# Transposes of a two-layer attention and token-MLP kernel, from the full array to four 64x64 tiles

## The chip, the core and the metric

The kernel runs on one core of a Trainium2 chip. The metric is the device time of one execution in microseconds (us). Engines are called as in the profile: PE is the matrix engine, DVE the vector engine, ACT the scalar engine that computes activations, POOL the general engine, SP the engine whose queue starts the loads. PSUM, where PE writes, has eight banks of 512 float32 per partition; bank numbers below are the second index of the tile `ps`.

## The reference

The input x has 2048 tokens of 512 features. Two layers, each of two halves, use the same weights twice:

```python
x = x + _A_ref(_layernorm(x), A_wqkv, A_wo)                # sliding-window attention
x = x + _B_ref(_layernorm(x), B_w1, B_b1, B_w2, B_b2)      # MLP across the tokens
x = x + _A_ref(_layernorm(x), A_wqkv, A_wo)
x = x + _B_ref(_layernorm(x), B_w1, B_b1, B_w2, B_b2)
```

`_A_ref` has 32 heads of 16 features; each token attends to itself and the 255 tokens before it. `_B_ref` multiplies along the tokens (2048 to 1792, gelu, 1792 to 2048) for each feature.

## The kernel before, in words

Tokens lie in 16 tiles of 128 (`x_sb`, and normalised `xh_sb`). Attention goes through four blocks Q of 512 tokens. A block needs its normalised tokens with features on the partitions, `xhT` (two buffers in turn). From it PE computes k, q and v in projections of four 128x128 by 128x512 matmuls (`project`, L591; v at L695). Then there are 36 steps a block (four groups of heads, nine shifts m of the window): `emit_scores` (L795) writes scores into one of two pairs of PSUM banks (0 and 1, or 2 and 3), `emit_exp` (L806) takes the exponential on ACT, an edge mask is multiplied in by DVE or POOL (L823), and `emit_pv` (L844) adds probabilities times values into banks 4 and 5. Scores and values use the array as four independent 64x64 tiles; such operations carry the mode "cells" in the code, the others "full".

All other products of PE during attention share banks 6 and 7: projections, transposes, the normalisation of the output (L887), the output product (L760), and parts of the MLP that are done beside attention (L607). A product occupies its bank from the write until the instruction that empties it has ended.

The first block's four token tiles are transposed one at a time (L567). The later blocks' tiles are transposed in pairs by `job_transpose_two` (L580): two jobs for each of three blocks in each of two layers, twelve jobs in all. One job is eight transposes of 128x128 against the identity, written as bf16 into one bank (8 x 128 x 2 bytes fill it), and one copy of 128x1024 from there to `xhT` (`copy_out`, L440 on DVE or L442 on ACT).

The order of work is written out by hand in tables. The program records operations as jobs, sorted by due time and then put in the sequence `ORDER`; dependencies (who must wait for whom, through tiles and banks) follow from that sequence. `BANKS` has bits for each job that choose bank 6 or 7 for each product. `LINES` gives each engine its list of operations, by their number among all operations in job order, so it also says which engine does an operation that several could do. Each engine runs its list strictly in order (`Plan.emit`) and waits on semaphores where a dependency is on another engine. PE therefore stops at a product whose bank is not yet empty, and all behind it on PE stops too.

Of the kernel before, what the change touches and what calls it, by code (L numbers as in the profile page):

```python
# [29 lines left out]
def _table(*text):  # L30
# [5 lines left out]
    'c-pm-Ne;ju3<DYe|It<36QUtoiNu9qWIOQ~ckvvCUEkdu!hhkTGe1YTP~@rQU0fFp^)x;4x-$AF=Njp%un%%{$-(R<s119<{N!Zp&wOBPJZ2gw'  # L36
    '_#DUKdY*TM)IMraJ>OSnL0d(ACotVqnr}=Y&BW*Olgl)%J+933^`8{tWL?s+0Cx')
ORDER = _table(
    'c-jTQ17Hvc00q#G>{_;$ZQEM5ZQHnPo6ELs+qP}qdjKJXM+g|95E5aK5^)h0kr5i<5E0Q40Z|YM(U1_a5EU^I196Z5fry9Lh>v7Qj6}$YBuIgz'
    'NQ2}^g|x_l)JTU+$d86dkF3ao?8uB_$c1dkgPh2K0OUh%6ht}XMPU>`Q4~TE)I~{@MsZX{36w=CR74q+M<wh-5UQXlDx*58p%yxzChDLDx}gGU'  # L40
    'qdpp=I~t%KnxPR|U?TdWC7Pf$nxidRp$*!jGlrlO+My%5peuS}9@e8bMxh7#qZbCD9|mGHrei1uU^up+4+di-{=*22#TbmoZVbZ&Ou;xD!emUt'
    'RLsO|%)%VZ#SARKB+SPmEJQGt;sh3BIhJ81R^cqxVhuK6HP&GXHen;SVg){9Gqzv{wqqB*;4=1OC-&k14&pwJ;4qHiDQ@5tj^YeX;yCu;JWk^r'
    'F5(jI;R3EAB(LBauHz4G;}-7VChp=P9^eVy;5i=S5uV{CUg0&~;sqk{15)!nKH?odAt}G(D}Lh}e&Hv`4EzBw1pgrnO))gXGXk?R3L`T*OEQ45'
    '7@N^pkx?0!aTt*aS%V1}pNW}_F&K`Cn1m@9ipiOZe-X%(OvAKH$Mg)#{EWve%*f2l#9WNY?99fT%)=ba&AiOVRxHQ@EW*NU$YLDDLM+PSEWu7J'
    '%~CAOaxB9N3}Sg!VI|gLW!7X}R%dNCU>(+DBQ|DzR%J6bXHzy|OSWKJwr3l5VLNtaNA_TEc4K$;Vm}UGPj+Qr4&p!#<zNnDAO6RYoX9a8!PXqd'
    '(HzV1oWRMP!v37eX`IU0oWWU~$N8MZxm?60T*$>-%3!YGYA)wWuHrhb<$7-CHE!TlZsc_i;R5dAGG5^(?&frE;Z5G=X0G8a-rx>y<xXznF7D+%'
    'p5y`U=P4fMSsv$69^?fc;|ZST5uW2Ap5aBF=Oy0ZWj^LzKHz;m;ypg(dp_fHzTi`S<P*N+8@}Z$zUDiA;3t0JAAaR`M$<Qb<}ZfV4~EcB{w4K~'
    'zZpjs6iQM^g;p3vRX9adVue*?MNlN=RSX3vtD-2n;wh$LDYfD%ff6acnkcCfD!Gy<nF3W#sZ>)Ll}<&JM(LGZnbl93ludb*LpfDnxm8g4)k#y8'
    'PlZ)L#Z*W=)LNxgROMAll~h(0RasS3O+yr0HB?o#Rb91IR}EE1jnzQS)JRR$LM@d`DV0H4lveH3M$HwZR_dU(YOgZttZwR}3hJto>aG&%rM~K|'
    '0qUc{>aRf>rjDwo5gMxD8m)mErLh{L@tUC7nxtu3pk<n<8JeP5>Z$3PsX3afd77`)TC9aSpkOW4a;?xv?b0f()EceTIIY(@ZPX@h&=zghHf`52'  # L50
    '?a)r`(QfV4WbM--ZPh^?)(IWaQ61N5oz!`q(J5WjSzXX2UDge~*A?B>65Y{l-PAK(*EQYO13l7H-O@RQ@I$@OW4+Z?J<)T$)JMJ1Ywgz;z0(JM'
    ')=z!XJ^j`Xebq1h(>KBLEB#eS({^ZwaeRkzIEQsaf7c&HaU@4@fFnDaqdTUPI)-CAj^jDJqdJx2I*}7Ni4!`pW4Vk2oy;kn+&P`W>73eWT*zIW'
    '!kL`jX`R&>oyB!r#krls&79r2T*P^t*L_^rrCiL#o!R+a!j)Xs*__YiT+!7X<kGI}f-dTkuIXy7=kl)M`mXDSZsaCz>I!b*R&L|gZtsq6;M#8M'
    '4sPx)uIldY?4IuC9`5DdZs*4C?|vTW0dDCb9_GOw>7gFs;U4309__In?+Kpd$?ofEp5m#V=^38o*<R!W-tRfy>p@=XQQqfep6iL8=fghe`JV1W'
    'KH?=_=mlQvV6XCKZ}Cbm_X=<IHt+NvZ}cXw_Xe-=TCesluk#LX_imr`d7tqmAN4U`^>Lr_37_^2pYuhZ^=)79Jzw!P-}hx-_Z{E#1K;&6KlCF%'
    '_7ndP&4=a!')
LINES = {
    "tensor": _table(
    'c-jrshkFRt769;j?>Xn5dv22ojaH4KjVDIZMA1GJv4a>-(HfPg5yYO!vqzMo)>C_ab`ce|pAa>kM6H_PqgIOw5<!T({t>_LS5bwkN~*G|qN=Je'
    '6|O#35h_wORne-Nicu|8JJnjXQD3M&DnTWw8ETZ8ppw;EHD66p^VA}>O6^e#)i$+KZB!f7Nwq^AP+QecYM(l!Zm1*bjC!JutBdM_%2J|ltE=iy'  # L60
    'bxWO4)72yOhssrD^-J}a%2A|Wr~=hk7uE0TNL@+?>Eb#>m((BXP+duf>)tv{SJ$8DT6&`Xr;gI|bzR+3ch?JaU)@5->4Ey9UaNcQ;W|kV(8F}1'
    '9;=gesve^!>uGw9UZ!(&1+z+T)JODEy;7&>4SJhCs_*EZ^?qI5?9gd?pFXHFb%s8p>zVWVy6$GK>EHED{fB<2|J2#~vCh|5^h;f+-)J_@3^0Kv'
    'zyzDpCdrgH<xHpvF<`2iDkjndnJg1wJ~cH>9dq4uG__3=)7f+}TTCzWjp=Lln?+`*8EN{MA;!QsGs28DlgwnZ*~~Gs&3yA8^TaGOOU+8N!E}IB'
    'v%~B$8Rn4LZPLs!bKIOXr%W+8Z_b&E=8|awcg=cuWbT*;Cf~$Cp?P5}6c~a)cpC=6`%nVPL0JfeN^lgyAq?umC8z-npgDMmg2vDaVxS#7Gyj4w'
    ';VbA0U&Azrg#OSQ5+EMNKnRS0p^yZfa3Una1egNJU~v}Agt>4ZR=^xs4y$1el)z1}5q7~r*aBN29kxLVWWshh1Bc-!$bt+w4OihN?0{6b2RGmj'
    'JcPgCH59;8$bnn{RQL>nFb{(9ITXRt_zsrB7Z8Fkp%Q+Cp%{U+u`JfZy4VaGVhaqzcGwXUFb+Fl0QSUK?1Ayv2NN*~Be5EOg4J;<j>8&Q6F<ez'
    'a0ZUWWc&_i<2)RQOK=dbz{R*62jdzXf~#>e4#i=Zg2QnWZo>n(AJgy=9>NiL7;`We8{q=X#&tLmJ)On^e1mUMCceOzn1$ysA8+7AEW{!dK#%bm'
    '22oK`^aS(p6_%zl6iUHVj*3xn3ZxQLiK<c<g-``5Pw!I%MbhWghU!uSYDm%4oZ8Y58cP4B(G*90DS^6EFN&vuG>XR40GdD}X(p|u*|dPNXg;l='
    'leC!j(sJ5N+v!JILuh}d6#6giqyu!A(&-8vqf=De{zgYBlg?5<dyjsnCf3=@beA5`LkhQS18p%IU@zD*wuCKe-?OFdhjx*zY<Jo^wx%6xtJ_+('
    'xs9@+T;ImqXxqxRw#V&I+uIJXc{Y)!*d*KE4zVL`Nxoy}*`;=}t--79T)WV&vg_>z`<R~47Q5X(r5|k$<<c|SZSyF_?y}G61*O}Uluy6fefAZ-'  # L70
    'rUE)=uh>)eti5b+*qgSU{ld1l9c)MYrTxl2wD)W$+u3%pUG3Mln~k-P?QQ$OX4}^`m<z1pzo|0tdyGtMxg1wuX2<1O*z;Q)z*RVqt8oZd=18u?'
    'x%Q}y;@VuFqdA<LaVw7D_S}`HavYE5xxA6bb1aYI$y|oV@g$zc(|Hzu&%1aLFXUWa%j<Xxr*I>_$*H`9_wjyi%V~U&kMVI%=L|l{m-sS+%i?Q%'
    'n{V+w?!i4dn|pC@e#P<Jhx>9qJ6Fj4SUGkH+@A+<5%;be$b)z=mvV2rcU(#Lfh+66TqpOLtKq7-aM#@Z!!>YCU9g+wVqBE#;2OIS*V4tg_U<Y7'
    'cCoIP8|>=15pIwh?#8-gH{G>$bKNvI(=Bj6xMOaKTkKZ31efU6yX|hJTjx^TPPfaQcL!XWJK~nRO)lMKx-%}ropyU&ExGP4xohsS3zl4$?e4n='
    'uA*#`=Pp1VxjcswFCC<m6qPX&BvquOd?00Iztoh<^07onzI)|jq`K6R*Y0yEa4jWP+Q=K%P72-MSxAEPkZ$sg43vH{REEhYNt6aMUcQrt(n!9S'
    '#xhG5N)u@+YowV(%RE^k>!piqmz}asQY2M&%O068|C1B)tDKSvGEpYUMVTyFazUoZEx9T;Bv~HFRQXo2<-R<Ur;;Q2@=6X$nkaur4ojf~`T!r~'
    ')1|0CBELv6e^g?8C*RGVmAlf)=SgQD>&y6NKH8V_b$vY_;Vb$$|B<ii8~WzHwQuAb`})3%@8Mhco<7RQ`|f_2Z{x@NuD*#M?)&&revqHw6Mcdo'
    '?ECxCevDt>SNo;@2fxA3@H72vKgVzNYy2{w>Ua9RexFbC8~rwa#Q)-t`$Im%XZq9ryg%cA^C$dOf64zJNC^?W'),
    "vector": _table(
    'c-jTQ3seYJ7y#h^{`da(zxOht)uxD&!iXhVGnGSyvYkp|4MQ=^BU2-(jTm`tEU$^fI+*9qMw93`DAPG(^dO{ZUd`-`J?z2k`#ORz_(3P=0xv)Z'  # L80
    '@PW4A30@Ed{h&XDLl{KB02l-w5Dk&w4}-xQ0^l_m2t(jScphRP7P`VP2!sSkfkc=JqoEk`Ar+=W8q9!PcnfC1A{Yw`U<?$%n=lS`!FZSeyI~)c'
    'z(hC(r{FYXKsuy|lW-GKMY4DViJ}@-LXsFQ#)u}k3thx0ktUwO6BsLEMW~3wAmJy1#YpTW#);Q)f_O&^#{psl7KtbkEe45UxI_#U@pwffV1r1+'
    'H*mhl6`5kL*d>mLLh-vu!S$k21mWi*825_<;*Ka26{0^T<7qJ(YeY1@jg#<!_(j|ox5RaEO*|C>XQM+e^u{^35OZ-6DkKa+jqNZK8?illVgwfA'
    'a%{p#T#E-W9am!pj>i*Nfm`rH+>gsp%15{pci?v1i>3G-o<UEUD&yo;tip@<0Ds0`@d-|nLK>MVJ*2PfD9_3OxkvVu4KiG|lC5Qe{1YEznhceN'
    'vY(tS^JJJ@Dd)*7*-fsJ`SJr9B!lG!xk;v}0=Zm%Ebq(D<fpP&7Re6EN9~tKWtps$M`Wq2l`XPP3WbW4xB6H9BVSTol)oCOLexyvMm?t@)T?Tp'
    '`a~6}Vs${BRxv78ZB%ipTJ2U#)E;$FeW41}CACQ{Rh!jeRjMwi^Xix?SB>h1s#Q&@PTf?^s$Tu5uBZleRozl|lplFhPYR(R3LqZ}r6`J~!8DX&'
    'D3;<Wi4tfeCDT00qHG#Psgy#CXe{MXKFy>VG?}JSI%Uu_%A_2cLyKtvt)X4CgbHXKEv1jBk&0+D?VuG@PFv|X71JRieV9t<BvsNi^48T<L$&m-'
    '{)ui=oF1lI={~xx_RyDgR~@Lg=+4?#m+E}oOGoP7Izji~A$q7z)aUeLou#vN4rl85dV%)kJGw}3(BZsIcjQC*gg&l?{*Rs!YN<gt>Ki&;Pt+ND'
    'lAf%mXm4JrSLn5Rjc&v3xILfMp4^r_xDWT`cwWxyc`xU&A9v<ue3Z-h7$4+A9K&C6EGKa?kK$8Y!DqOcFR(I|+`>(KkK_0uSMeqOo`2waM$^i)'
    'HtkFn&*f}>kNwR&exHkZJ4cu>6K{geKvTkAX1LkO1I!LyYr2`=c(RE!gUkme-z1wPv&wvH&Y5a6)66m@X12*O3r()6Gi9d2)SJuZmT5Mp%yv^{'  # L90
    '%1w(IXuWKW`NMR#4@?ic&uTl(PPeJHlg+ce?Fn09U$FtUs|~b?HpxcWXp44^&9vEewH;xL?N&S9j<a9eZ)}m>U^m)wd(}4EoA$OXv@7gG`_xM3'
    '>CW03TWfusue)m>+d6yCc6NTQ#r|dgw%RG@?*g22*1hbyyHMA|1-hQDn+tNiT|XD%`nYfx=BBu8H{C6EIc~0-<?`Gnx5lk=C2pH5b;sRa_ob_H'
    'r`&m0?=HD&cilC({{fr%KFI'),
    "scalar": _table(
    'c-jTQd1x187y#h!J-+w&z?GV;bfy^^ZN{jTQ*0&kkILCh87UoF6H^;%q&ew_xDuN%rFoR)F~%I^RkV@0B(=##iaKSqFl7mvw9I2hBhfK>o>5_1'
    'C=Ij1qR<lRLRDB2GGSx*I8=wv!uHS*_Jwc5>F`}R8rnl=I3K!0f~(<LxE1=s-5@X!hCnvtz*xwIe0U3<fyqz|FT;G;1{Lrgtb`1#foj+cbx;Eh'
    'un(HxXE+2$pcOix6T09MT!CwF8}30s$1EI)WAJf&0-wT(ScG%%P27MBu>x1%Dy+hFxEVjkI^2r~@h~38lXw=pupNKHKk*jc!$3;+(QtZ%aw(sl'
    'r$U-aB{YM|=rx*0OKCAxQij%2H7S2eTd1BIX+Ql$ZPY=X)J>PEhi=jUF%RZpJd($9E<ejt_$8jsWju$=`5k_jGrW|mcs+0At-O=#xseZW6CdS^'
    'T*<4rjZbk4|HXeZ#DDld?&nc)Xv~gTF)!xF$Ks=LL@bC;$2a1pxGmPl9r1MhIyT2c@mOq&C*s-oYwU?vqRWjqRI=nDd06tKND8Gyie<69A}eH>'
    'WaJasD!XL2?3HHuMt+bsIVZo!MY$|Dq(^ScFddKwwN}RHI32GATBLnatkZOc&ed0SwwCK^{Yckojn?XR?bENcNe}7~ZPk-{Mla~^dR2S1U){jE'  # L100
# [242 lines left out]
def bass_interleave_layers__sliding_block__mixer_token_mlp__prompt_kernel(  # L343
# [25 lines left out]
    with es:  # L369
# [202 lines left out]

        def job_transpose_two(Q, i, prio):
            b, t, buf = misc_bank(), 4 * Q + i, Q % 2
            pv = ps[:, b, :].bitcast(dt.bfloat16)

            def f(e):
                for j in range(2):
# [581 lines left out]
```

## Time and profile before

| What | us |
|---|---|
| Median of 3 runs | 504.71 |
| Lowest and highest | 503.58, 505.14 |
| The profiled execution, its own time | 504.01 |
| Its span (first to last instruction of the program) | 502.3 |
| L795 on PE, scores, 2816 matmuls | 108.5 busy |
| L844 on PE, values, 2816 matmuls | 92.1 busy |
| L580 on PE, the changed transposes, 96 matmuls | 7.1 busy |
| L806 on ACT, 288 exps | 261.5 busy |

Busy time counts stretches in which at least one instruction of the group ran; matmuls overlap, so for PE the distance from one start to the next says more than the length of one. The granted clock of PE is 0.999 of full speed throughout. Attention of layer 1 lies from about 14 to 163 us of the span, its MLP to 231 (with its last part beside the next attention), attention of layer 2 to 404, its MLP to the end.

### The profile page before, as it was taken

The numbers are of one execution on the slowest core, as the hardware profiler recorded it, in microseconds if no ns is written. First come the engines' busy times: TensorE is split into PE (matmuls) and PEld (weight loads), VectorE is DVE, ScalarE is ACT, GpSimd is POOL, SyncE is SP. The second block draws the span as 40 slices with busy tenths as digits, with TensorE's granted clock in tenths as the row PEclk, the third lists the DMA queues.
The fourth block names the chain that finished last, engine by engine and source line by source line (L and its number), as shares of the span: only waits on it lengthen the run. The fifth ranks groups of instructions, "written<-read, shape, count | busy, mean of one in ns | idle before, by whom it ended". The sixth has DMA issues, their size and how long they took to land.

```text
span 502.3 us, 19381 instructions
## 1 busy us (share of the span) xinstructions
PE 474.3 (94%) x8385; PEld 272.0 (54%) x8454; DVE 323.4 (64%) x660; ACT 315.6 (63%) x381; POOL 213.1 (42%) x375
## 2 busy tenths in 40 slices
PE   8898989998999999998998999999999999999997
PEld 4454556555766444444444776566547754444444
DVE  7989988887663571366897447878886549131222
ACT  2898999997999314400776669889989960340000
POOL 5897756664564030001874555577544312200000
PEclk9999999999999999999999999999999999999999
DMA  6922222242222725050002140114214256050661
GB/s 209 96 79 84 70 71 77 85 114 68 78 62 70 216 79 147 0 147 1 24 9 61 50 137 15 38 61 136 85 47 114 71 156 185 0 146 12 198 200 52
DMA packets 76516, 44.52 MB, mean 89 GB/s; under 512 B 8976, under 2 KB 75408, under 8 KB 76432
## 3 DMA queue, kind: packets, MB, share of 16 engines
q1 hardware_dynamic: 72560, 43.27, 29.3%
q0 software_dynamic: 3872, 0.02, 1.4%
q8 instruction: 66, 1.08, 0.9%
q14 instruction: 18, 0.15, 0.1%
HBM read 32.51 MB, written 2.10 MB: 69 GB/s over the span
## 4 chain that ended last, share of the span: by engine, by line
PE 70%; ACT 8%; DVE 6%; POOL 6%; issue 4%; DMA 3%; SPq 2%; DVEq 0%; ACTq 0%; POOLq 0%
PE ps L1029 14%; PE ps L983 13%; PE ps L795 9%; PE ps L844 8%; ACT p_sb L806 7%; PE ps L591 7%; PE ps L607 7%; PE ps L760 4%; PE ps L695 4%; POOL p_sb L823 3%; SPq L434 2%; PE ps L519 1%; PE ps L887 1%; DMA w1buf<-in_B_w_dram 1%; POOL xh_sb L544 1%
## 5 line engine op out<-in xcount | busy, mean ns | idle before, releaser
L806 ACT ACTIVATE p_sb<-ps 128x1024 bf16<-128x1024 f32 (+8 forms) x288 | 261.5, 977 | 47.4 <-PE ps L795 39.0
L823 POOL TENSOR_TENSOR p_sb<-p_sb,edge 128x128 bf16<-128x128 bf16 (+2 forms) x263 | 127.4, 491 | 114.1 <-ACT p_sb L806 99.3
L795 PE MATMUL ps<-q_sb,k_sb 64*64 64x288 bf16 (+8 forms) x2816 | 108.5, 249 | 3.4 <-ACT p_sb L806 2.3
L844 PE MATMUL ps<-p_sb,v_all 64*34 64x288 bf16 (+17 forms) x2816 | 92.1, 246 | 4.4 <-issue 1.5
L795 PEld LDWEIGHTS ps<-q_sb,k_sb 64*64 64x64 bf16 x2816 | 60.0, 106 | 46.6 <-ACT p_sb L806 22.6
L844 PEld LDWEIGHTS ps<-p_sb,v_all 64*64 64x64 bf16 (+1 forms) x2816 | 60.0, 100 | 21.5 <-POOL p_sb L823 6.3
L591 PE MATMUL ps<-xhT,wqkv 128*128 128x512 bf16 x214 | 55.4, 380 | 4.8 <-issue 2.7
L823 DVE TENSOR_TENSOR p_sb<-p_sb,edge 128x128 bf16<-128x128 bf16 (+2 forms) x137 | 39.9, 300 | 21.9 <-ACT p_sb L806 14.5
L1033 DVE SCALAR_TENSOR_TENSOR x_sb<-ps,b2col,x_sb 128x512 bf16<-128x512 f32 x23 | 17.1, 750 | 44.4 <-PE ps L1029 43.9
L537 POOL TENSOR_TENSOR rstd<-vare,mhalf 128x4 f32<-128x4 f32 (+1 forms) x17 | 16.6, 977 | 67.1 <-DVE vare L535 53.9
L983 PE MATMUL ps<-xh_sb,w1buf 128*128 128x512 bf16 x186 | 44.1, 379 | 0.6 <-issue 0.5
L525 DVE BATCH_NORM_STATS2 stats<-x_sb 128x6 f32<-128x512 bf16 x64 | 43.0, 681 | 0.6
L710 POOL TENSOR_TENSOR v_all<-vt,even 128x1024 bf16<-128x1024 f32 (+2 forms) x23 | 34.3, 1495 | 17.3 <-DVE vt L698 17.3
L547 ACT ACTIVATE xh_sb<-x_sb,shift,rstd 128x512 bf16<-128x512 bf16 x11 | 8.8, 813 | 50.5 <-POOL shift L541 34.7
L632 DVE TENSOR_TENSOR k_sb<-ps,half 128x1024 bf16<-128x1024 f32 (+1 forms) x32 | 37.3, 1166 | 4.7 <-PE ps L622 2.4
L1029 PE MATMUL ps<-ubuf,w1buf 128*128 128x512 bf16 x165 | 37.4, 379 | 0.2
L607 PE MATMUL ps<-xh_sb,w1low 64*64 64x512 bf16 x512 | 35.5, 377 | 0.1
L1029 PE MATMUL ps<-ubuf,oU 128*128 128x512 bf16 x150 | 34.5, 379 | 0.2
L988 DVE TENSOR_TENSOR ps<-ps,ubuf 128x512 f32<-128x512 f32 x16 | 11.2, 700 | 35.1 <-PE ps L983 35.1
L591 PEld LDWEIGHTS ps<-xhT,wqkv 128*128 128x128 bf16 x240 | 19.5, 98 | 26.5 <-issue 4.4
L695 PE MATMUL ps<-xhT,wqkv 128*128 128x512 bf16 x114 | 30.1, 380 | 3.5 <-issue 1.4
L990 ACT ACTIVATE ubuf<-ps,b1col 128x512 bf16<-128x512 f32 x28 | 19.0, 686 | 22.9 <-DVE ps L988 13.0
(89 smaller groups left out, 531.4 us busy)
## 6 DMA issues: line engine op xcount, KB each, us to landing
w1buf<-in_B_w_dram SPq DMA_DIRECT2D x30, 256.0 KB
w1buf<-in_B_w_dram SPq DMA_DIRECT2D x50, 128.0 KB
oU<-in_B_w_dram SPq DMA_DIRECT2D x18, 256.0 KB
oU<-o SPq DMA_DIRECT2D x16, 256.0 KB
w1low<-in_B_w_dram SPq DMA_DIRECT2D x32, 128.0 KB
q_sb<-qt SPq DMA_DIRECT2D x120, 32.0 KB
xhT<-in_B_w_dram SPq DMA_DIRECT2D x4, 512.0 KB
k_sb<-in_B_w_dram SPq DMA_DIRECT2D x4, 512.0 KB
```

Source lines behind the costliest of these rows:

```text
L525: dve(lambda e: e.bn_stats(stats[:, t, :], x_sb[:, t, :]), 690, prio, reads=[R("x", t)], writes=[R("stats", t)])
L591: last = e.matmul(ps[:, b, :], lhsT=wqkv[:, c, c0:c0 + P], rhs=xhT[:, buf, c, :], start=(c == 0), stop=(c == 3))
L607: last = e.matmul(ps[64 * h:64 * h + 64, banks[r ^ swap], :], lhsT=lhs(r ^ swap, c, rows, 64 * h), rhs=rhs(r ^ swap, c, rows), start=(c == ...
L632: return e.tensor_tensor(dst, src.unsqueeze(2).to_broadcast([P, n, 2, w]), mask[:].unsqueeze(1).unsqueeze(3).to_broadcast([P, n, 2, w]), o ...
L695: last = e.matmul(ps[:, b, :], lhsT=wv[:, c], rhs=xhT[:, buf, c, :], start=(c == 0), stop=(c == 3))
L710: return e.tensor_tensor(dst, src.unsqueeze(2).to_broadcast([P, n, 2, DH]), even[:].unsqueeze(1).unsqueeze(3).to_broadcast([P, n, 2, DH]), ...
L795: last = e.matmul(ps[64 * c:64 * c + 64, 2 * half + r, 32 * i0:32 * i1], lhsT=k_sb[rows, ring, t, kb % 16, :], rhs=q_sb[rows, t, c, 32 * i ...
L806: exps[plan.job] = last_exp[0] = plan.op({ACT: (170 + int(2 * (512 - c0) * 0.84), lambda e: e.activation(p_sb[:, slot, :, c0:512], ps[:, 2 ...
L823: return e.tensor_tensor(v, v, g, op=ALU.mult)
L844: last = e.matmul(ps[64 * r:64 * r + w, B_O + (c ^ r), 32 * i0:32 * i1], lhsT=v_all[rows, pos - 32 * c:pos - 32 * c + w], rhs=p_sb[rows, s ...
L983: r = e.matmul(ps[:, b, :], lhsT=blk[:, sc - 8 * part, (ft % 2) * P:(ft % 2 + 1) * P], rhs=xh_sb[:, sc, :], start=(sc == 8 * part), stop=( ...
L1029: r = e.matmul(ps[:, b, :], lhsT=blk[:, turn[n], (st % 2) * P:(st % 2 + 1) * P], rhs=u_at(turn[n]), start=(n == 0), stop=(n == NFT - 1))
```

## The change

`job_transpose_two` transposes in quarters of the array. For each of the eight 128x128 pieces there are now four transposes of 64x64, one for each row half r and column half h, in the position (64r, 64h) of the array. Row half r writes to its own bank, so a job takes both shared banks, and uses half of each. Each bank is emptied by a copy of 128x512; the two copies can go to different engines. The job's mode is "cells".

```diff
         def job_transpose_two(Q, i, prio):
-            b, t, buf = misc_bank(), 4 * Q + i, Q % 2
-            pv = ps[:, b, :].bitcast(dt.bfloat16)
+            banks, t, buf = (misc_bank(), misc_bank()), 4 * Q + i, Q % 2
+            pv = [ps[:, b, 0:256].bitcast(dt.bfloat16) for b in banks]
 
             def f(e):
                 for j in range(2):
                     for c in range(4):
-                        last = e.transpose(pv[:, (4 * j + c) * P:(4 * j + c + 1) * P], xh_sb[:, t + j, c * P:(c + 1) * P], ident[:])
+                        for r in range(2):
+                            rows, n = slice(64 * r, 64 * r + 64), 64 * (4 * j + c)
+                            for h in range(2):
+                                last = e.transpose(pv[r][64 * h:64 * h + 64, n:n + 64], xh_sb[rows, t + j, c * P + 64 * h:c * P + 64 * h + 64],
+                                                   ident[rows, rows], tile_position=(64 * r, 64 * h))
                 return last
-            pe(f, 450, prio, reads=[R("xh", t), R("xh", t + 1), R("ident")], writes=[BK(b)])
-            copy_out(xhT[:, buf, :, i * P:(i + 2) * P].rearrange("p c (j n) -> p c j n", j=2),
-                     pv.rearrange("p (j c n) -> p c j n", j=2, c=4), b, prio, 750, [R("xhT", buf, i), R("xhT", buf, i + 1)])
+            pe(f, 240, prio, reads=[R("xh", t), R("xh", t + 1), R("ident")], writes=[BK(b) for b in banks], mode="cells")
+            for r, b in enumerate(banks):
+                copy_out(xhT[:, buf, :, i * P:(i + 2) * P].rearrange("p c (j r n) -> p c j r n", j=2, r=2)[:, :, :, r],
+                         pv[r].rearrange("p (j c n) -> p c j n", j=2, c=4), b, prio, 420, [R("xhT", buf, i + r)])
```

The numbers 450, 240, 750 and 420 are the planner's costs in ns; with the tables given they do not act. The tables `BANKS`, `ORDER` and `LINES` are replaced whole. Decoded, they say:

- PE's list has 1004 operations before and after, the same ones; 621 keep their relative order. DVE has 648 operations in place of 660, ACT 381 in place of 372, POOL 386 in place of 371, SP 375 as before.
- Before, the jobs' copies are 11 on DVE and 1 on ACT; after, 21 on DVE and 3 on ACT.
- Counting the new jobs as "cells", PE's list goes from "full" to "cells" and back 100 times before and 90 times after.
- The next product in one of a job's banks, counted in places of PE's list: before, at least 4 places after the job for every job; after, 3 to 5 places for nine jobs, and 6 or 7 for the other three.
- In layer 2, ACT's list has 191 operations in place of 181; in layer 1, 190 in place of 191.

## Prediction, on record before the result was known

> **What bounds the kernel now.** I read the page's engine table first, then the chain of work that ended last, then busy time by stage (before attention, attention of layer 1, its MLP, attention of layer 2, last MLP).
>
> ```profile
> span 502.3 us, 19381 instructions
> ...
> PE 474.3 (94%) x8385; PEld 272.0 (54%) x8454; DVE 323.4 (64%) x660; ACT 315.6 (63%) x381; POOL 213.1 (42%) x375
> ...
> PE 70%; ACT 8%; DVE 6%; POOL 6%; issue 4%; DMA 3%; SPq 2%; DVEq 0%; ACTq 0%; POOLq 0%
> ```
>
> TensorE is busy in 94% of the span and holds 70% of the chain. So work that it no longer does is worth nearly its length, wherever it is not waiting for another engine.
>
> ```profile
> 14.00:163.00 149.00, 138.69 (x3440) 85.62 (x3467) 117.03 (x241) 137.23 (x162) 95.30 (x165) 1.00 0.32 80
> ...
> 231.00:404.00 173.00, 163.62 (x3866) 104.50 (x3893) 126.92 (x248) 138.60 (x161) 93.91 (x161) 1.00 0.22 64
> ```
>
> These are the two attention stages, where all twelve changed jobs lie (columns: length, PE, PEld, DVE, ACT, POOL, granted clock, DMA). In layer 1 PE (138.7) and ACT (137.2 of 149.0) are both nearly full; in layer 2 ACT has 34 us to spare. PE idles 10.3 + 9.4 us in the two.
>
> One changed job in the timeline of PE (start, length, line):
>
> ```profile
> 41.94 0.39 PE L795 MATMUL ps<-q_sb,k_sb 64*64 64x288 bf16 x8
> 42.26 0.62 PE L580 MATMUL ps<-ident,xh_sb 128*128 128x128 bf16 x8
> 42.81 0.30 PE L844 MATMUL ps<-p_sb,v_all 64*34 64x256 bf16 x4
> ```
>
> The job holds PE for 0.55 us from its first start to the next instruction's.
>
> **TensorE's price, from start to start.** Busy times of pipelined matmuls overlap, so I take the records' starts. Eight 128-column transposes start 56 ns apart (median of 119): 8 x 56 = 0.45 us a job. A group of four 64x64 matmuls, one on each quarter of the array, takes 28 ns for 64 columns (145 groups) and 56 ns for 128 (221). The new job is 8 such groups of 64 columns: 8 x 28 = 0.22 us. The saving is 0.224 us a job, 12 jobs: **2.7 us**. The trace has no eight short groups in a row, only single ones between longer ones, so the other end is the 56 ns that the rows of 16 groups at L887 keep up, at which this term is zero. I take 28, since the row has the same tile and the same columns.
>
> The Trainium skill speaks against this. "TensorE: Matmul & The Clock Gate", section "Wait — 56ns, not 53.3ns?", says that matmuls never start closer than about 25 ns, however small. Counted for each of the 32, that is an estimated 0.80 us a job, and the sum below would turn to a loss of about 2 us before any wait. The trace bears it out for groups only: the four matmuls of a 64-column group start within 10 ns (median), and 32-column groups still take 28.
>
> **Changes of mode.** Between quarter tiles and the full array PE loses time beside the pitch: quarter to full 158 ns after a 128-column group, against 56; full to quarter 149 after a transpose, against 56, and 309 after a 512-column matmul, against 216. A pair costs 0.10 + 0.09 = 0.20 us. I decoded the order tables in the diff and walked PE's list: 100 pairs before, 90 after (54 to 51 in layer 1, 46 to 39 in layer 2), since every new transpose job stands between attention steps, which use quarter tiles. 10 x 0.20 = **2.0 us**. Together PE has 4.7 us less to do: 6 x 0.224 + 3 x 0.20 = 1.94 in layer 1 and 2.74 in layer 2.
>
> **Copies.** One copy of 1024 becomes two of 512.
>
> ```profile
> L440 DVE COPY xhT<-ps 128x1024 bf16<-128x1024 bf16 x11 | 7.4, 679 | 0.9 <-PE ps L580 0.9
> ...
> L440 DVE COPY xhT<-ps 128x512 bf16<-128x512 bf16 x6 | 2.4, 415 | 1.5 <-PE ps L567 1.4
> ...
> L442 ACT ACTIVATE xhT<-ps 128x512 bf16<-128x512 bf16 x2 | 1.2, 597 | 7.8 <-PE ps L567 7.8
> ```
>
> The tables put 21 on DVE and 3 on ACT. DVE: 21 x 0.415 - 11 x 0.679 = +1.2 us; ACT: 3 x 0.597 - 1.045 = +0.7. DVE is idle for 78 us in the two stages, so the work as such is hidden; if that cover were gone it is 1.2 us. The new copies write runs of 64 elements in place of 128; no row shows that. The nearest row has the same size, 0.415, which I take; the far end is the 0.679 of twice the size, which would add 5.5 us to DVE's work and 0.5 to each wait below (in the range by rival 1).
>
> **The wait that is added.** Each job now holds both shared banks until both copies are done. After its first start: last group 0.20, copy begins 0.26 later (42.66 to 42.92 at the job above), two copies in turn on DVE 0.83, hand-over 0.09 (a DVE transpose ended at 345.01, PE's waiting transpose started at 345.10): both banks are free at 1.38 us, the first at 0.96 (1.15 if ACT copies it). Before, one bank was held for 0.41 + 0.26 + 0.68 + 0.09 = 1.44 and the other was free. The next user of a bank comes early in the new list. An attention half-step (scores, or values) holds PE for 0.22, so at n places after the job PE arrives at 0.22 n:
>
> - n = 3, both banks or the second, three times (layer 1 third block, layer 2 second and third): 1.38 - 0.66 = 0.72 each
> - n = 3 and 4 with the bank that ACT copies: 0.49 and 0.27
> - n = 4 with the second copy's bank, twice: 0.50 each; with the first's: 0.08
> - n = 5, 6 and 7: 0.28, 0.06, 0.12 (at 7 another product stands between the copies on DVE)
>
> Sum **4.5 us**; the same working for the old list gives 0.1. PE is in order, so the attention behind it waits, and with it the exps on ACT.
>
> ```profile
> 343.41 3.77 ACT L806 ACTIVATE p_sb<-ps 128x1024 bf16<-128x1024 f32 x4 [0.68 <-PE ps L844]
> ...
> 343.77 0.62 PE L580 MATMUL ps<-ident,xh_sb 128*128 128x128 bf16 x8
> ...
> 345.11 0.62 PE L580 MATMUL ps<-ident,xh_sb 128*128 128x128 bf16 x8
> ```
>
> Not all of it is on the path. Here two jobs of before stand four places apart, and PE took 1.34 us from one to the other while ACT ran four exps without a gap. Where ACT sets the pace, a step takes 1.03 us however fast PE is, and a wait of 0.5 lies inside it. The bounds are 0 and 4.5; with ACT full in layer 1 and four fifths full in layer 2, I take half: **2.2 us**.
>
> **The rest of the order.** Two fifths of PE's places change, and as many or more of those of DVE, POOL and SP's loads. In layer 2 ACT gets ten instructions more (191 against 181), eight of them in the first quarter of that attention (243 to 281 us), where it was busy 27.8 of 38 us; without that cover they are some 7 us, at 0.6 to 0.8 apiece. The edge products that change engine (72 from POOL to DVE, 84 back) stand beside DVE's idle 78 us. Loads keep their number and sizes. I count this at nothing. It can gain or lose part of the 19.7 us that PE idles; I allow 1 us below for it.
>
> **Sum.** 2.7 + 2.0 - 2.2 = 2.5 us. The profiled execution took 504.01 (span 502.3 and 1.7 around it), giving 501.5; the median shown is 504.71, 0.7 above it, and so **502.2**.
>
> **Rivals.**
>
> 1. Copies come late (slower). The copies queue behind other work: at the third job of layer 2 the tables put a layer-norm statistic (0.68) ahead of them on DVE, and where ACT copies, an exp (1.03) can. With half of a 0.7 us instruction ahead at each of the eleven places and no wait hidden: 4.5 + 3.9 = 8.4 lost against 4.7 won, **508.3**. It decides from 4.7 on, that is from about 0.2 us of queue a place if half of the 4.5 is hidden. For it: DVE is 73 to 79% busy there. Against: the list puts the copies early. The Trainium skill has the mechanism in general: "TensorEngine Tiling (Array Packing)", "PSUM Bottleneck", says that tiling speeds up TensorE but not the emptying of PSUM. The trace agrees: 0.22 us of transposes, 0.83 of copies.
> 2. The waits count in full, no queue: 4.7 - 4.5, **504.5**, no difference.
> 3. ACT sets layer 1: its 1.94 is lost; layer 2 keeps 2.74 less half of its 2.3 of waits = 1.6, **503.1**, on the edge of what can be told.
> 4. Short groups in a row take 56 ns: 2.0 - 2.2, **504.9**, no difference.
> 5. The four matmuls of a group do not start together, each takes the 28 of a group: 32 x 28 = 0.90 us a job, 12 x 0.45 = 5.4 lost, with 2.0 won and 2.2 waited 5.6, **510.3**. The starts within 10 ns speak against it. The floor on starts in the Trainium skill, cited above, would act in this way.
> 6. The new list also fills idle time of PE: under **500.0**, all of the 4.7 or more.
>
> **How the numbers follow.** Forecast 0.38 (its own range 500.0 to 503.2), rival 1 0.27, 2 0.10, 3 0.10, 4 0.05, 5 0.03, 6 0.07. A measurement here tells 0.3% (1.5 us) from no change. Faster: 0.38 + 0.07 + half of rival 3 = 0.50; same: 0.05 + 0.10 + 0.05 = 0.20; slower: 0.30. The range goes from 499.0 (all of 4.7 and 1 us of idle time) to 508.3; above lie half of rival 1 and rival 5, 0.165, below half of rival 6.
>
> **What would show it.** In the new profile: 384 transposes of 64x64 whose groups start 28 ns apart (or 56, or worse); 90 pairs of mode changes at 0.20; 24 copies of 128x512 near 0.415 on DVE; PE waiting for the xhT copies at the places named, 4.5 us in the sum if nothing hides them. PE's idle time in the two stages should stay near 19.7 + 2.2. The prediction is wrong if that idle time grows by over 4.7 us, or if PE's busy time does not fall.

## The result and the profile after

| | before | after |
|---|---|---|
| Median | 504.92 (503.58 to 506.26, 4 runs) | 499.84 (499.27 to 500.58, 4 runs) |
| Ratio, with its 95% interval | | 0.990 [0.9870, 0.9931] |
| The profiled execution, its span | 504.01, 502.3 | 499.27, 497.3 |

The change saves 5.1 us, twice the 2.5 forecast; 499.84 lies inside the stated range (499.0 to 508.3), near its lower end. The page of the new kernel, its span, engine table, chain and the queue that brings the instructions (packets, MB, share):

```profile
span 497.3 us, 19993 instructions
...
PE 471.8 (95%) x8674; PEld 270.8 (54%) x8742; DVE 325.6 (65%) x648; ACT 321.0 (65%) x396; POOL 218.7 (44%) x390
...
q8 instruction: 69, 1.13, 1.0%
...
PE 73%; POOL 8%; ACT 6%; DVE 5%; issue 5%; DMA 2%; SPq 0%; ACTq 0%; POOLq 0%; DVEq 0%
```

PE is as full as before and its share of the chain rises from 70 to 73%. Its busy time is a poor measure here, though: 8674 of 8742 matmuls have a record, and a second profile of the same kernel, with all of them, has 481.8 us busy. So I compare starts. Before's page lacks about as many (69 of 8454). As far as the two can be compared, neither of the prediction's signs of being wrong appears: PE's busy time falls from 474.3 to 471.8, and between the first and the last exp of the two attentions PE idles 18.3 us before and 17.9 after. It did not gain the 2.2 us that the prediction added.

The new operations (by form: count, then busy us and mean ns of one, then the idle time before them):

```profile
L440 DVE COPY xhT<-ps 128x512 bf16<-128x512 bf16 x27 | 10.5, 417 | 2.6 <-PE ps L583 1.7 <-PE ps L567 0.6
...
L583 PE MATMUL ps<-ident,xh_sb 64*64 64x64 bf16 x384 | 5.3, 194 | 0.5 <-POOL v_all L715 0.2
...
L583 PEld LDWEIGHTS ps<-ident,xh_sb 64*64 64x64 bf16 x384 | 4.4, 109 | 1.7 <-DVE xhT L440 0.9 <-issue 0.4 <-DVE k_sb L637 0.2
...
L442 ACT ACTIVATE xhT<-ps 128x512 bf16<-128x512 bf16 x5 | 3.0, 601 | 2.6 <-PE ps L567 2.0 <-PE ps L583 0.6
```

And the first two jobs in the timeline (start, length, operation; in brackets the idle time before it and what ended it):

```profile
30.03 0.43 PE L583 MATMUL ps<-ident,xh_sb 64*64 64x64 bf16 x32
30.28 0.37 PE L849 MATMUL ps<-p_sb,v_all 64*34 64x288 bf16 x8
...
30.55 0.76 DVE L440 COPY xhT<-ps 128x512 bf16<-128x512 bf16 x2
...
31.36 0.33 PEld L583 LDWEIGHTS ps<-ident,xh_sb 64*64 64x64 bf16 x32 [0.16 <-DVE xhT L440]
31.36 0.45 PE L583 MATMUL ps<-ident,xh_sb 64*64 64x64 bf16 x32
```

The job holds PE for 0.25 us (30.03 to 30.28), where the one of before held it for 0.55. Its groups of four start 31 to 32 ns apart. The two copies together take 0.76 us, and the second job comes when they are done: 31.36 is 1.33 after the first job's start, close to the 1.38 that the prediction had for "both banks free". PE's waits for the xhT copies of the new jobs, as idle time of its weight loads, line by line (sum in us, times, longest):

```profile
PEld ps L583 <- DVE xhT L440: 0.9, 3, 0.4
PEld ps L700 <- ACT xhT L442: 0.8, 2, 0.5
...
PEld ps L892 <- DVE xhT L440: 0.4, 1, 0.4
```

With two more of 0.2 these are 2.5 us, not 4.5. It is an upper bound: matmuls may still run in that time, and the matmuls' own rows have 0.35 us of waits for xhT copies.

**Where the time went.** The 288 exps on ACT are the same in both kernels, in the same order, so the start of each is a clock: first exp of layer 1, its last (number 144), first of layer 2, its last, end of the span.

| us | start | attention 1 | between | attention 2 | end |
|---|---|---|---|---|---|
| before | 15.28 | 148.24 | 75.99 | 166.65 | 96.12 |
| after | 14.88 | 146.43 | 74.03 | 165.75 | 96.18 |

Attention of layer 1 gives 1.8 us, that of layer 2 0.9, and 1.96 come from the stretch between, where no changed job lies. One trace is not enough for the 0.9: a second profile of the changed kernel (changed_again) has 146.45 and 74.03 again, but 166.81 in layer 2. PE in before, at the end of the first MLP (timeline):

```profile
229.93 0.62 PE L567 MATMUL ps<-ident,xh_sb 128*128 128x128 bf16 x8
232.39 1.05 PE L622 MATMUL ps<-xhT,wqkv 128*128 128x256 bf16 x8 [1.84 <-DVE xhT L440]
233.49 2.10 PE L1029 MATMUL ps<-ubuf,oU 128*128 128x512 bf16 x9
```

and in after:

```profile
227.79 0.61 PE L567 MATMUL ps<-ident,xh_sb 128*128 128x128 bf16 x8
228.23 2.32 PE L1034 MATMUL ps<-ubuf,oU 128*128 128x512 bf16 x9
230.39 1.91 PE L627 MATMUL ps<-xhT,wqkv 128*128 128x256 bf16 x16
```

These are the unchanged single-tile transposes of layer 2's first block, its first k product (L622, in after L627), and the MLP's last output product (L1029, L1034), which needs nothing of that block. Before, the k product stood first and waited 1.84 us for the copies; the new list puts the MLP product there, and the wait is gone.

### The profile page after: what moved, and what is told of

It is laid out like the page before. It is cut to its first block, busy times and chain, and to the rows that moved or that the text cites. A ratio compares the mean times of both kernels' runs of the same rounds, so it can differ in the third digit from the quotient of the medians.

```text
span 497.3 us, 19993 instructions
## 1 busy us (share of the span) xinstructions
PE 471.8 (95%) x8674; PEld 270.8 (54%) x8742; DVE 325.6 (65%) x648; ACT 321.0 (65%) x396; POOL 218.7 (44%) x390
## 4 chain that ended last, share of the span: by engine, by line
PE 73%; POOL 8%; ACT 6%; DVE 5%; issue 5%; DMA 2%; SPq 0%; ACTq 0%; POOLq 0%; DVEq 0%
PE ps L1034 14%; PE ps L988 14%; PE ps L612 10%; PE ps L800 9%; PE ps L849 9%; PE ps L765 6%; ACT p_sb L811 5%; PE ps L596 5%; PE ps L700 3%; POOL p_sb L828 2%; POOL v_all L715 1%; POOL rstd L537 1%; PE ps L519 1%; PE ps L892 1%; POOL xh_sb L544 1%
## 5 line engine op out<-in xcount | busy, mean ns | idle before, releaser
L828 POOL TENSOR_TENSOR p_sb<-p_sb,edge 128x64 bf16<-128x64 bf16 (+2 forms) x275 | 132.5, 490 | 105.5 <-ACT p_sb L811 82.4
L849 PE MATMUL ps<-p_sb,v_all 64*34 64x288 bf16 (+17 forms) x2816 | 94.4, 246 | 5.6 <-POOL p_sb L828 3.5
L849 PEld LDWEIGHTS ps<-p_sb,v_all 64*34 64x34 bf16 (+1 forms) x2816 | 60.7, 100 | 26.2 <-POOL p_sb L828 11.3
L828 DVE TENSOR_TENSOR p_sb<-p_sb,edge 128x256 bf16<-128x256 bf16 (+2 forms) x125 | 42.3, 344 | 29.6 <-ACT p_sb L811 23.3
L537 POOL TENSOR_TENSOR rstd<-vare,mhalf 128x4 f32<-128x4 f32 (+1 forms) x17 | 17.7, 1044 | 83.2 <-DVE nmean L539 61.4
L1034 PE MATMUL ps<-ubuf,w1buf 128*128 128x512 bf16 x163 | 37.3, 379 | 0.3
L637 DVE TENSOR_TENSOR k_sb<-ps,half 128x1024 bf16<-128x1024 f32 (+1 forms) x29 | 34.5, 1197 | 3.8 <-PE ps L596 3.2
L1034 PE MATMUL ps<-ubuf,oU 128*128 128x512 bf16 x151 | 35.0, 379 | 0.2
L596 PEld LDWEIGHTS ps<-xhT,wqkv 128*128 128x128 bf16 x240 | 19.7, 97 | 26.0 <-issue 2.1
L547 ACT ACTIVATE xh_sb<-x_sb,shift,rstd 128x512 bf16<-128x512 bf16 x8 | 6.4, 811 | 38.8 <-POOL shift L541 38.8
L765 PE MATMUL ps<-wo_sb,oT 128*128 128x512 bf16 x116 | 29.5, 380 | 1.7 <-issue 1.4
```

The costliest lines, as they stand in the source:

```text
L596: last = e.matmul(ps[:, b, :], lhsT=wqkv[:, c, c0:c0 + P], rhs=xhT[:, buf, c, :], start=(c == 0), stop=(c == 3))
L637: return e.tensor_tensor(dst, src.unsqueeze(2).to_broadcast([P, n, 2, w]), mask[:].unsqueeze(1).unsqueeze(3).to_broadcast([P, n, 2, w]), o ...
L765: last = e.matmul(ps[:, b, :], lhsT=oT[:, buf, t, i * P:(i + 1) * P], rhs=wo_sb[:, t, :], start=(t == 0), stop=(t == 3))
L828: return e.tensor_tensor(v, v, g, op=ALU.mult)
L849: last = e.matmul(ps[64 * r:64 * r + w, B_O + (c ^ r), 32 * i0:32 * i1], lhsT=v_all[rows, pos - 32 * c:pos - 32 * c + w], rhs=p_sb[rows, s ...
L1034: r = e.matmul(ps[:, b, :], lhsT=blk[:, turn[n], (st % 2) * P:(st % 2 + 1) * P], rhs=u_at(turn[n]), start=(n == 0), stop=(n == NFT - 1))
```

## The experiments

Theory after the result: the gain is the short job (PE's 4.7 us less some waits) plus the new order, which takes out the 1.84 us wait. Rivals: the order alone made it; two banks or shorter copies made it. Medians are compared with runs of before made together with them; the kernel as changed was run once more as well.

| kernel | median | before | ratio [95%] |
|---|---|---|---|
| new_order_old_job | 502.68 | 503.76 | 0.9980 [0.9962, 0.9997] |
| old_order_short_job | 503.80 | 503.76 | 0.9994 [0.9978, 1.0010] |
| full_two_banks | 502.37 | 503.76 | 0.9976 [0.9958, 0.9993] |
| late_copies | 509.97 | 503.76 | 1.0130 [1.0096, 1.0163] |
| changed_again | 500.47 | 504.76 | 0.9916 [0.9891, 0.9941] |
| double_transposes | 508.84 | 504.76 | 1.0091 [1.0061, 1.0121] |
| work_behind | 508.10 | 504.76 | 1.0069 [1.0046, 1.0091] |
| old_order_one_move | 502.66 | 504.76 | 0.9962 [0.9946, 0.9978] |
| wide_group | 501.71 | 503.99 | 0.9954 [0.9931, 0.9978] |
| row_tiles | 500.00 | 503.99 | 0.9922 [0.9898, 0.9947] |
| masks_on_dve | 499.21 | 503.99 | 0.9897 [0.9869, 0.9926] |
| change_without_move | 501.50 | 504.44 | 0.9946 [0.9929, 0.9962] |

### The parts of the change, one by one

**new_order_old_job**: the new tables, with the job of before (eight 128x128 transposes into one bank, one copy).

> The new order tables with the old job: eight 128x128 transposes into one bank, one copy of 1024 (the list entry of the second copy is dropped). PE's list then changes between full and quarter array 102 times in place of 90, and a job holds PE 0.55 us plus 0.10 to enter, in place of 0.25. Theory 1, PE's saved work counts at its length and the order is worth nothing by itself: 12 x 0.40 = 4.8 us slower than the changed kernel, 504.6, no difference from before. Theory 2, the new order brought the gain by leaving PE idle less: about 500, 1% faster than before. Half and half: 502.

0.9980. The stretch between the layers is 74.04, as in the change. By the medians the kernel gains 1.1 us, so the order with the old job wins 1.95 us there and gives nearly half of it back elsewhere. (In the profiled execution attention 2 is 168.24, 1.6 longer than before, but that execution took 504.86, 2.2 over its median.)

**full_two_banks**: new tables, two banks and two copies, but 128x128 transposes.

```diff
-                        for r in range(2):
-                            ...
+                        last = e.transpose(pv[j][:, c * P:(c + 1) * P], xh_sb[:, t + j, c * P:(c + 1) * P], ident[:])
```

> The changed kernel as it is (order, two banks, two copies), but with 128x128 transposes: the four of a token tile go into one bank. Theory 1: PE pays 12 x 0.20 for transposes and 12 pairs of mode changes more, 2.4 + 2.4 = 4.8 us slower than the changed kernel, 504.6. Theory 2: about 500. If the two banks and two copies cost something that one bank does not, it is slower than the new order with the old job, by up to the 4.5 us of waits that the prediction counted; if they are hidden, the two are equal.

0.9976, not to be told from the single bank's 0.9980. Taking both banks, and copying twice, costs nothing that can be seen; by the intervals, up to about 1 us could hide. From here to the change only the tiles differ: 0.9976 to 0.990 and 0.9916 in its two series, 0.6 to 0.8%, or 3.0 to 3.8 us. That is what the short groups and the saved mode changes are worth in this order. On PE they are 2.35 us (eight groups, see below) and 12 pairs of mode changes: PE's list has 102 pairs here against 90, and the traces of the two attentions have 199 single changes against 175.

**old_order_short_job**: the old tables and one bank. It transposes only the first 64 tokens of each pair of tiles, in eight groups of two 64x64 tiles, and copies those values, in two instructions, to the places of the other 64 as well; the second half is left out.

```diff
-                        last = e.transpose(pv[:, (4 * j + c) * P:(4 * j + c + 1) * P], xh_sb[:, t + j, c * P:(c + 1) * P], ident[:])
+                        for h in range(2):
+                            n = (4 * j + c) * P
+                            last = e.transpose(pv[64 * h:64 * h + 64, n:n + 64], xh_sb[0:64, t + j, c * P + 64 * h:c * P + 64 * h + 64],
+                                               ident[0:64, 0:64], tile_position=(0, 64 * h))
```

> The old order tables, with a job as short as the new one: only the first 64 tokens of each tile are transposed, in two 64x64 tiles at a time, into one bank; the copy fills the other 64 tokens with the same values (two instructions of 512 in one operation, so the bank is held about 0.1 us longer). So the result of the transpose is not the reference's. PE has 12 x 0.20 us less of transposes and 8 pairs of mode changes less (92 for 100), 1.6 us. Theory 1: 4.0 us faster than before, 500.9, and no new order needed. Theory 2: 504.9, as before, since the time is in the order.

0.9994: a job as short on PE gives nothing that can be told in the old order (1.1 us at most by the interval). Counted from each layer's first exp, the exps get 0.8 us ahead of before's in layer 1 and 1.5 in layer 2, and all but 0.2 of each lead is gone when the layer ends. Where it goes, PE's waits for the copies of `o` are 1.3 us (0.9 before) in layer 1 and 0.6 (0.2 before) in layer 2, with 0.5 each for two other operations of DVE (`vt`, `stats`) that before does not show there. After has no wait for `o` from 0.2 us up. That these waits belong to the old list is likely and not shown; which of its entries would make them I did not settle. The two-bank job could not be tried in the old PE list: a k product's bank is emptied there by work that stands behind the job.

### The one move

**old_order_one_move**: the kernel before, with one entry of PE's list moved: the first ten matmuls of the MLP's output tile 7 ahead of the first k and q products of layer 2.

> The kernel before, old order and old job, with one entry of PE's list moved: the first ten matmuls of the MLP's y tile 7 of layer 1 go ahead of the first k and q products of layer 2, where PE waited 1.8 us for the copies of the first block. The trace of before has the wait there (230.5 to 232.4 us) and every kernel with the new order has none. If the order's whole worth in the middle of the kernel (75.9 to 76.0 us between the exps 144 and 145 with the old order, 74.0 with the new) is this move: 1.9 us faster than before, 0.996. If the new order needs its other moves there too: less than 1 us.

0.9962 (-1.9 us) and 74.10 for the stretch between, against 75.99. The gain of that stretch, 1.9 us, is this move.

**change_without_move**: the change, with the same entry put back behind the first two k products.

> The changed kernel with one entry of its PE list put back behind the first two k products of layer 2: the first ten matmuls of the output product of y tile 7 (2.3 us of PE work that needs none of the copies of the block). Nothing else differs, and nothing is left out. Theory 1, the order's gain in the middle stage and the short job's gain add up: PE waits again about 1.8 us for the copies of the block's xhT, the middle stage goes from 74.03 back to about 75.9, the other stages stay, and the time is 1.5 to 2.0 us above the change (ratio to before about 0.994 to 0.995). Theory 2, the short job needs just this move to gain anything (in the old order it gave nothing): the loss is 3 us or more, and the ratio is 0.998 or above. Theory 3, the wait moves to a place with slack: the time stays within 0.5 us of the change (0.990 to 0.992).

0.9946; the stretch is 75.89 again, and the wait is back (timeline; the k product has line 549 here):

```profile
229.60 0.61 PE L489 MATMUL ps<-ident,xh_sb 128*128 128x128 bf16 x8
231.86 1.05 PE L549 MATMUL ps<-xhT,wqkv 128*128 128x256 bf16 x8 [1.66 <-DVE xhT L362]
```

Theory 1 of this expectation holds: the move adds to the rest. The change without it keeps 0.54%, 2.9 us by the medians.

### What would have made it slower

**late_copies** is rival 1 as a kernel: ahead of each xhT copy on DVE stands a reduction of the bank that it empties.

```diff
             def on_dve(e):
+                e.tensor_reduce(extra, flat, axis=mybir.AxisListType.X, op=ALU.max)
                 return e.tensor_copy(dst, src)
```

> The changed kernel, with one more instruction of DVE ahead of each copy on DVE: it reduces the 512 elements of the bank to one column (about 0.5 us), so each bank is held longer and DVE has 21 x 0.5 = 10 us more work. Theory 1, the holding of the banks is hidden beside attention with room to spare: under 1 us slower, 500 to 501. Rival, the holding is on the path (the prediction's rival 1): both banks are held 0.5 to 1.0 us longer in each of some 9 places, 4 to 9 us slower, 504 to 509.

```profile
L456 DVE TENSOR_REDUCE scratch<-ps 128x1 bf16<-128x512 bf16 x21 | 14.3, 683 | 1.8 <-PE ps L596 1.6
```

The 21 reductions are 14.3 us of DVE's work, and the kernel takes 1.3% more than before and about 11 us more than the change. In its profiled execution (514.44) PE's matmuls wait 9.0 us for xhT copies, in nine waits, where after has 0.35. The largest row (us in all, times, longest):

```profile
PE ps L596 <- DVE xhT L457: 5.0, 5, 1.3
```

**work_behind** has the same 21 reductions, of a constant tile, behind a job's last copy on DVE, so that they hold no bank.

> As late_copies, with the same 21 further reductions of 512 elements on DVE (0.7 us each, about 14 us), but behind the job's last copy on DVE, on a tile that nobody waits for: the banks are held no longer than in the changed kernel. If late_copies was slow because the banks were held (1.3 us longer a job), this is within 3 us of the changed kernel. If it was slow because DVE is full, this is as slow as late_copies, 11 us above the changed kernel. In between, both count, each by its part.

1.0069, 7.6 us over changed_again, though PE waits only 1.2 us for xhT copies. So the same work on DVE is dear either way: held banks stop PE in late_copies, and without them DVE's load delays other operations that PE waits for (3.8 us for DVE's `p_sb`, `oU` and `o`, against 0.8 in changed_again). The difference of the two runs, about 3 us, is therefore not the price of holding the banks. DVE is busy in 65% of the span, and still about half of 14 us more has no cover.

### What the tiles cost

**double_transposes** does each transpose twice, into the same place.

```diff
-                for j in range(2):
+                for j in range(4):
```

> The changed kernel with each transpose job's 32 matmuls issued twice with the same values, so PE has 12 x 8 x 32 ns = 3.0 us more in the same mode and the banks are written 0.25 us later. Theory 1, PE's work counts at its length: 3.0 us slower than the changed kernel. Theory 3, formed from the four runs before: attention is paced by chains through several engines, and about half of what PE spends or saves in a job arrives at the end: 1.5 us slower. Under 0.5 us would mean that PE has slack there and only the mode changes counted.

For 12 x 8 x 31.5 ns = 3.0 us more of PE's work it takes 8.4 us more than changed_again. The rest is in stops of PE, most of them within the matmuls of one operation, where no semaphore is waited for. Two of them, in jobs at 63 and 252 us (timeline of PE):

```profile
62.67 0.70 PE L583 MATMUL ps<-ident,xh_sb 64*64 64x64 bf16 x62
65.19 0.22 PE L583 MATMUL ps<-ident,xh_sb 64*64 64x64 bf16 x2 [1.82 <-issue]
...
251.69 0.48 PE L583 MATMUL ps<-ident,xh_sb 64*64 64x64 bf16 x36
253.02 0.41 PE L583 MATMUL ps<-ident,xh_sb 64*64 64x64 bf16 x28 [0.85 <-issue]
```

The profile calls the releaser "issue": PE waited for no operand and no bank that the profile shows, so its instructions may not have been there. Measured from one start to the next, there are seven such stops of 0.8 to 2.0 us, 8.2 us in all; changed_again has two (2.9 us), before three (2.3), and the rest of the kernels none to three. Theory 4 from here on: many short instructions close together outrun their supply.

**wide_group** adds about as much PE time with few instructions: ahead of each job one group of four 64x64 matmuls of 512 columns, 12 x 0.216 = 2.6 us.

```diff
+                for r in range(2):
+                    rows = slice(64 * r, 64 * r + 64)
+                    for h in range(2):
+                        e.matmul(ps[64 * h:64 * h + 64, banks[r], :], lhsT=ident[rows, 64 * h:64 * h + 64], rhs=xh_sb[rows, t, :],
+                                 start=True, stop=True, skip_group_check=True, tile_position=(64 * r, 64 * h))
```

> The changed kernel with one more group of four 64x64 matmuls ahead of each job's transposes, of 512 columns, into the same two banks (the transposes then write over it): 12 x 0.216 = 2.6 us more of PE with 8 instructions more a job. The doubled transposes had 3.0 us more of PE with 64 instructions more a job, and lost 8 us; their trace has seven pauses of PE of 0.8 to 2.0 us within an operation, where no semaphore is waited for, against two in the changed kernel, and three more 16 KB packets on the instruction queue. Theory 4, PE's instructions arrive too slowly for runs of short matmuls (a packet of 256 each 3.3 us at the closest in every trace): this kernel loses no more than its PE time, 1.3 to 2.6 us, with 2 or 3 pauses. Rival, the place is sensitive to anything longer in a job, whatever it is made of: 7 us.

0.9954: by the ratios 1.9 us (give or take 1.7) over changed_again for 2.6 of work, and its trace shows no stop of that kind. So the number of instructions, not the time, made double_transposes dear. The 0.7 us for each us of PE's work is a mixture, no price: in the profiled execution layer 1 is 0.7 longer than in after, layer 2 0.3 longer although after's stop of that kind is missing, and 1.06 come from the stretch between, where PE waits once, 1.0 us, for `oT`.

**row_tiles** transposes in two tiles of 64x128, each with half as many instructions.

```diff
-                            for h in range(2):
-                                last = e.transpose(pv[r][64 * h:64 * h + 64, n:n + 64], xh_sb[rows, t + j, c * P + 64 * h:c * P + 64 * h + 64],
-                                                   ident[rows, rows], tile_position=(64 * r, 64 * h))
+                            last = e.transpose(pv[r][:, n:n + 64], xh_sb[rows, t + j, c * P:(c + 1) * P], ident[rows, rows],
+                                               tile_position=(64 * r, 0))
```

> The changed kernel with the transposes in two tiles of 64 rows by 128 columns in place of four of 64x64: the same banks, the same columns and copies, but half the instructions (32 in place of 64 a job, the old job had 16). By theory 4 it relieves the supply of instructions: up to 1 or 2 us faster than the changed kernel, with fewer pauses. Against it: if a change between tiles of 64x64 and of 64x128 costs what one to the full array does, 12 x 0.20 = 2.4 us slower, half of it or all. Equal to the changed kernel if neither counts.

0.9922, as the change in the median. In the trace it is not the same (timeline of PE, third job):

```profile
58.46 0.41 PE L582 MATMUL ps<-ident,xh_sb 64*128 64x64 bf16 x16
58.79 0.41 PE L848 MATMUL ps<-p_sb,v_all 64*34 64x192 bf16 x12
```

Its groups of two start 29 ns apart, but the job holds PE for 0.33 us, against 0.27 at the same place of after. From its last matmul to the next 64x64 one it is 120 ns, where after has 9 to 22 at the places without a wait; ahead of its first matmul, such places have 0.10 to 0.12 us more than after. So going from 64x64 to 64x128 tiles and back costs about what going to the full array does. Over the twelve jobs PE spends 1.2 us more than in after. Layer 1 is 0.9 us longer, and layer 2 is 1.0 shorter, where the trace lacks the stop of 1.6 us (start to start) that after has at 343 to 345 us. The equal medians can be these two together; whether fewer instructions help is not settled.

### A version a little further

**masks_on_dve**: the largest wait of after's values for POOL is at the start of layer 2, where five edge products stand behind a normalisation on POOL (timeline):

```profile
238.76 1.75 POOL L544 TENSOR_SCALAR xh_sb<-x_sb,rstd,shift 128x512 bf16<-128x512 bf16 x2
...
240.49 1.72 POOL L828 TENSOR_TENSOR p_sb<-p_sb,edge 128x64 bf16<-128x64 bf16 x5
...
241.49 0.41 PE L849 MATMUL ps<-p_sb,v_all 64*34 64x288 bf16 x8 [1.36 <-POOL p_sb L828]
```

Two of the five go to DVE, which is idle there.

> The changed kernel with two list entries moved: the two edge products (64 and 128 columns) of layer 2's first step go from POOL, where they stand behind two normalisations (238.8 to 240.5 us), to DVE ahead of its two normalisations. The trace of the changed kernel has PE waiting 1.4 us for them (240.1 to 241.5) and ACT idle 0.7 after. If a delay at one place is carried to the end, as the exps' times of all runs suggest, 0.7 to 1.3 us faster than the changed kernel; if another wait takes its place at once (the third step's edge products stay on POOL), no difference.

PE's waits of this kind, first in after, then here (L771 is L849):

```profile
PE ps L849 <- POOL p_sb L828: 3.5, 8, 1.4
```

```profile
PE ps L771 <- POOL p_sb L750: 2.1, 7, 0.5
```

The long wait is gone. The exps of layer 2 get 0.8 us ahead of after's within the first six and are 0.7 ahead at the end (165.03 in place of 165.75). 499.21, 0.9897 [0.9869, 0.9926], is the lowest ratio here, but it can't be told from the change's 0.990 and 0.9916.

## Why the prediction was right and wrong

- **Transposes, 2.7 us**: right, a little too large. Eight groups in a row start 31 to 32 ns apart, not 28; 12 x 8 x (56 - 31.5) ns = 2.35 us. Rivals 4 (56 ns) and 5 (28 for each matmul) fall with that, and with rival 5 the reading that the floor on starts in the Trainium skill ("TensorE: Matmul & The Clock Gate", "Wait — 56ns, not 53.3ns?") holds for each of four tiles.
- **Mode changes, 2.0 us**: the change between quarter tiles and full array costs in after what it did before (158 against 56 ns, 309 against 216), and the traces of the two attentions have ten pairs fewer. From full_two_banks to the change it is 12 pairs, with the transposes 4.7 us of PE; 3.0 to 3.8 of them come through in the time. The prediction counted PE's saved work at its full length.
- **Copies**: right. 417 ns with runs of 64 elements, against 415; two in a row take 0.76, not 0.83.
- **The added wait, 4.5 us, half of it counted**: the size looks right (at most 2.5 us of waits, against 2.2), and that is luck. I charged it to the two banks, but new_order_old_job, with one bank, has 2.6 us of the same waits, full_two_banks 2.8 (idle time of the weight loads), and their medians do not differ. The waits come with the new order, and whatever they cost is already off its gain of 1.1 us. As a price of the two banks the term should have been about nothing, and rival 2 falls with it.
- **The rest of the order, counted at nothing**: the step that failed. It took out 1.9 us at a place that the trace of before shows: the wait of 1.84 us from 230.5, PE's longest for an xhT copy. It stood third among PE's waits from 14 to 404 us (us in all, times, longest):

```profile
PE ps L622 <- DVE xhT L440: 1.8, 1, 1.8
```

1.4 us of it, behind 231, are even in the 19.7 us of idle time that the prediction counted and set at nothing. What it did not do is look up what the new list puts at that place. Decoding what stands between the four transposes and the first k product would have given the term. Against it, the order loses about 0.9 us elsewhere (new_order_old_job gains 1.1 in all).
- **Sum by the runs**: order 1.1, two banks 0.2, tiles 3.0 to 3.8: 4.3 to 5.1, as in the two series. The agreement proves nothing, since each part is the difference of two runs in a row. The forecast missed by 2.6 and 1.8 in the two: 1.9 for the move and 2.2 for the wait, less 0.9 to 1.7 of PE's 4.7 that does not come through and about 0.9 that the order loses, is 1.5 to 2.3.
- **Rival 1** has a real mechanism: in late_copies PE waits 9.0 us for xhT copies. Its 508.3 was for half an instruction of 0.7 us ahead of the copies; late_copies has a whole one ahead of each and takes 509.97, so the price itself was not tested. In the change little queues: a job's first copy begins 0.25 to 0.48 us (median 0.28) after the job's last start, 0.26 at the job that the prediction shows.
- **Rival 3**: ACT does not set layer 1, which became 1.8 us shorter of the 1.94 that PE saved there.
- **Rival 6**, with a chance of 0.07, is half of what happened. The new list does fill idle time of PE, at a single wait, but 0.9 to 1.7 of PE's 4.7 us do not come through; 499.84 is just under its 500.0, and the second series (0.9916 of before) would be just above.

What stays open: why the old order gives a short job's gain away and the new one keeps most of it, and whether 64 short instructions a job already cost something in the change.

## What to carry to other kernels

When a change replaces a whole order, list the longest waits of the bounding engine over the entire span, and look up for each what the new order puts there: one entry of a list was worth 1.9 us here, about as much as the prediction gave all the saved mode changes. How much of an engine's saved time comes through depends on the order (3.0 to 3.8 of 4.7 us in the new one, nothing that could be told in the old), so measure the part in the order that it will run in. Split the parts by runs, since the sum alone would have hidden what banks, tiles and order each do, and read the trace of a run whose time does not move: row_tiles has two opposite changes in it.

## What the runs showed of the hardware

- **Instruction supply.** PE's instructions come in packets of 16 KB on the queue that the profile's page calls "q8 instruction": 66 in before, 69 in after, 72 in double_transposes. In the trace's records of that queue, one takes 0.9 to 2.0 us, and none starts less than 3.3 us after the one before, in any of these kernels. The seven stops above end 1.3 to 1.5 us after such a packet has ended (one ran from 62.3 to 63.7, and PE went on at 65.19). They do not come from the 3.3 us: the packet ahead of each stop began 4.1 to 13.9 us after the one before it. The times fit packets that come too late for a stretch of short instructions; the link is argued from them and from wide_group, not shown by itself, and what starts a packet no run shows. The Trainium skill, "Advanced Engine Details and Errata", section "ISA Cache", gives lines of 16 KB, 256 instructions each. The packets' size agrees, and their number nearly: the 8742 matmuls and 8742 weight loads of changed_again over its 69 packets are 253. The same stop is in after, in the middle of a group of values:

```profile
344.74 0.63 PE L849 MATMUL ps<-p_sb,v_all 64*64 64x224 bf16 x14 [1.31 <-issue]
```

- **Tiles in a row.** Eight groups of four 64x64 matmuls of 64 columns keep up 31 to 32 ns a group; 64x64 against 128x128 costs 0.10 + 0.09 us there and back, and 64x64 against 64x128 about the same (row_tiles: 0.10 to 0.12 in, 0.09 to 0.11 out, at places without a wait).
- **DVE's copies overlap.** Two of 0.42 us in a row start 0.33 apart and take 0.76 together.
